# Attention scores of two heads at once: the queries' lo part as two 64-row tiles of PE

## The chip, the cores and the metric

The kernel runs on one core of a Trainium2 chip. Its time is the device time of one execution in microseconds; lower is better. A profile is one more execution, recorded by the hardware profiler. Engines are named as in the profile: PE is TensorE's matmul, PEld its weight load, DVE VectorE, ACT ScalarE, POOL GpSimd, SP the queue that issues most DMAs.

## The reference

Four batches, eight heads, 576 positions, head dimension 64. Attention has a bias that a small network makes from positions; after it come a dense layer pair and a layer of eight experts. Only the first function meets the change:

```python
def _attn_ref(q, k, v, w1, b1, w2):
    B, H, S, D = q.shape
    scores = np.matmul(q, k.transpose(0, 1, 3, 2)) / np.sqrt(D)
    ...                                   # bias from positions, [H, S, S]
    scores = scores + bias.transpose(2, 0, 1)[None, :, :, :]
    scores = scores - np.max(scores, axis=-1, keepdims=True)
    attn = np.exp(scores)
    attn = attn / (np.sum(attn, axis=-1, keepdims=True) + 1e-09)
    return np.matmul(attn, v).astype(np.float32)

def reference(**kwargs):
    ...
    x = attn_out.transpose(0, 2, 1, 3).reshape(B * S, H * D)
    x = _moe_ref(x=x, **moe_kwargs)       # x @ w_in, leaky relu, @ w_out
    return _moe2_ref(x=x, **moe2_kwargs)  # argmax over 8 experts, relu(x @ w1) @ w2
```

## The kernel before

**Precision.** An operand that must be exact to f32 is split into a hi part (rounded to f32r) and a lo part, the rest. A product then takes hi x hi, hi x lo and lo x hi. For scores, the two heads of a pair lie in one tile `kt` of 128 rows: head 0 has hi keys in rows 0 to 63 and lo keys in rows 64 to 127, head 1 the other way round. The queries stand twice, in rows 0 to 63 and again in rows 64 to 127, as `qhi` and `qlo`. One matmul over 128 rows with `qhi` therefore gives hi x hi and hi x lo at once; one with `qlo` gives lo x hi, and lo x lo besides.

**Steps.** Work is cut into 32 groups (batch, half of the queries, pair of heads) and these into 80 steps of 128 queries; the last step of every second group holds 64 queries of both heads (`ib == 4`, tile `qtail`). The other 64 are ordinary steps. A step's stages are spread over the loop of `phase1` (L638 to L682): while step n has its probabilities transposed (`transposes`, L450: tile `pst`; `transpose_tail`, L466: `psx`), the scores of step n + 2 are made. After a group's last step `values` (L485, tile `psv`) multiplies by the values, in column tiles of 64 (`tile_position=(0, 64 * h)`).

**Scores.** `scores(st, h)` (L392) makes one head: two column halves of 288 keys, each qhi then qlo, in a buffer `pss` of two PSUM banks. There are two such buffers (pool `psS`). One DVE instruction (L412) scales, adds the bias that already lies in `prob`, writes `prob` back and keeps the row's extreme in `stat`; `exps` (L417) is ACT's exponential, `normalise` (L425) the division, on POOL, DVE or ACT by a table.

**Fillers.** Between the stages stand units of other work, handed out by `Filler.run` against a quota of time: in the first eight steps the bias network (`bias_units`, L237, tile `psb`, column tiles of 32: four matmuls beside each other), then the up projection of the dense layers (`up_units`, L507, tile `psh`, twelve full matmuls a unit). `side` starts loads and conversions of later groups and of the dense layers' weights (`w_raw`, `wo_raw`, whose three bit operations run on DVE, L97 to L103).

**Order.** The program's text gives the order only roughly: the framework's scheduler sets each engine's list of instructions by priorities and readiness, so a change of a few lines moves many others. From the first matmul of the down projection (`psx` of L762) on, the lists of both kernels agree on PE.

What stands between two heads' scores in the loop is this:

```python
        if nx:
            at.scores(nx, 0)
        ...                              # normalise, side, half of the filler
        if st[3] != 4:
            at.transposes(st, 1)
        if nx and nx[3] != 4:
            at.scores(nx, 1)
```

Of the kernel before, what the change touches and what calls it, by code (L numbers as in the profile page):

```python
# [7 lines left out]
F32 = mybir.dt.float32  # L8
# [6 lines left out]
ALU = mybir.AluOpType  # L15
# [25 lines left out]
HALVES = ((0, 256, (0, 1)), (256, 320, (2, 3, 4)))  # L41
# [72 lines left out]
def new_w_in(p):  # L114
    return [p.tile([128, KD, FF // 2], F32R, name=f"wi{k}") for k in range(2)]
# [166 lines left out]
class Attention:  # L282
# [105 lines left out]
        self.prob[st] = (bt, e.small.tile([128, 2, 2], F32, tag="stat", name="stat"))  # L388

    def scores(self, st, h):  # L392
        nc, e = self.nc, self.e
        b, hf, p, ib = st
        kt = self.kv[b, p]
        hi, lo = self.qs[b, hf, p]
        tail = self.qtail[0]
        pr, stat = self.prob[st]
        ps = e.psS.tile([128, 2, 512], F32, tag="s", name="pss")
        o = 128 * (ib - HALVES[hf][2][0])  # L400
        if ib == 4:
            ops = [(tail[:, 256 * hh + 128 * k:][:, :128], 640 * hh) for hh in range(2) for k in range(2)]
        else:
            ops = [(t[:, h, o:o + 128], 576 * h) for t in (hi, lo)]
        for jh in range(2):
            for k, (lhsT, c0) in enumerate(ops):
                nc.tensor.matmul(  # L407
                    ps[:, jh, :288], lhsT=lhsT, rhs=kt[:, c0 + 288 * jh:][:, :288],
                    start=(k == 0), stop=(k == len(ops) - 1),
                )  # L410
        prv = pr[:, h].rearrange("p (a j) -> p a j", a=2)
        nc.vector.tensor_tensor_reduce(  # L412
            out=prv, in0=ps[:, :, :288], in1=prv,
            scale=-0.125, scalar=3.0e38, op0=ALU.add, op1=ALU.min, accum_out=stat[:, 0, h:h + 1],
        )

    def exps(self, st, h):  # L417
        nc = self.nc
# [134 lines left out]
def phase1(ctx, tc, e):  # L553

    nc = tc.nc
    early = tc.tile_pool(name="early", bufs=1, side="left")
    e.bout = early.__enter__()
    e.late = None
    at = Attention(nc, e)
    fl = Filler()  # L560
    groups = [(b, hf, p) for b in range(B) for hf in range(2) for p in range(NP)]
    steps = [g + (ib,) for g in groups for ib in HALVES[g[1]][2]]
    ns = len(steps)
    start = {}
    for n, st in enumerate(steps):
        start.setdefault(st[:3], n)


    todo = {}

    def put(n, pos, f, *args):
        todo.setdefault((max(n, 0), pos), []).append((f, args))

    def side(n, pos):
        for f, args in todo.pop((n, pos), ()):
            f(*args)

    for k, g in enumerate(groups):
        b, hf, p = g
        n0 = start[g]  # L580
        if k >= 2:
            put(n0 - 5, 1, at.q_load, g)
            put(n0 - 4, 1, at.q_hi, g)
            put(n0 - 3, 0, at.q_lo, g)
        if hf == 1:
            put(n0 - 3, 1, at.q_split_tail, g)
        if hf == 0 and k >= 2:
            m = n0 - 4 if b == 0 else start[b - 1, 1, p] + 3
            put(m, 0, at.kv_load, b, p)
            put(m, 1, at.kv_hi, b, p)  # L590
            put(m + 1, 0, at.k_lo, b, p)
            put(m + 3, 1, at.v_load, b, p)

    for k in range(2 * KF):
        put(3 + k // 2 if k < KF else 12 + (k - KF) // 2, k % 2, w_in_split, nc, e, k // 2, k % 2)
    for k in range(2 * KF):
        put(20 + k, k % 2, w_out_narrow, nc, e, k // 2, k % 2)

    bias_setup(nc, e)
    bu = bias_units(nc, e, WIDE)  # L600
    for k in range(32):
        if k == 20:
            for g in groups[:2]:
                at.q_load(g)
                at.q_hi(g)
                at.q_lo(g)
            for p in range(2):
                at.kv_load(0, p)
                at.kv_hi(0, p)
                at.k_lo(0, p)  # L610
                at.v_load(0, p)
        next(bu)
    fl.add(bu)
    for n in range(4):
        at.load_bias(steps[n])
    loaded = 4
    for n in range(2):
        for h in range(2):
            at.scores(steps[n], h)
            at.exps(steps[n], h)  # L620
    at.normalise(steps[0])

    xs = prev = None

    def values_out():
        nonlocal prev, xs
        if prev is None:
            return
        pb, ph, pp = prev
        if pp == 0:  # L630
            pool = e.xp if ph == 0 else e.late
            xs = [pool.tile([128, KD, HALVES[ph][1]], F32R, tag=f"x{i}{ph}", name=f"x{i}", bufs=1) for i in range(2)]
        at.x_split(prev, *xs)
        if pp == NP - 1:
            fl.add(up_units(nc, e, pb, ph, *xs))
        prev = None

    for n, st in enumerate(steps):  # L638
        g = st[:3]
        b, hf, p = g  # L640
        first = start[g] == n
        last = st[3] == HALVES[hf][2][-1]

        quota = 40 * 800.0 / 6.5 if n < 8 else KF * 1600.0 / 8 if hf == 0 else (13 if b == 0 else 17) * 1280.0 / 12
        nx = steps[n + 2] if n + 2 < ns else None
        while loaded < ns and at.free:
            at.load_bias(steps[loaded])
            loaded += 1
        if first:
            at.new_group()  # L650
        at.transposes(st, 0)
        values_out()
        at.transpose_tail(st)
        if nx:
            at.scores(nx, 0)
        if n + 1 < ns:
            at.normalise(steps[n + 1])
        side(n, 0)
        fl.run(quota / 2)
        if nx:  # L660
            at.exps(nx, 0)
        if st[3] != 4:
            at.transposes(st, 1)
        if nx and nx[3] != 4:
            at.scores(nx, 1)
        side(n, 1)
        at.done(st)
        if n == 7:
            fl.drain()
        else:  # L670
            fl.run(quota / 2)
        if nx and nx[3] != 4:
            at.exps(nx, 1)
        if last:
            at.pop_group(g)
            if n == 7:
                early.__exit__(None, None, None)
                e.late = ctx.enter_context(tc.tile_pool(name="late", bufs=1, side="left"))
                e.wi.append(new_w_in(e.late))
                at.free.append(PROBS)  # L680
            at.values(g)
            prev = g  # L682
    at.x_split(prev, *xs)
    fl.add(up_units(nc, e, prev[0], prev[1], *xs))
    return fl
# [661 lines left out]
def program(tc, e):  # L1347
# [4 lines left out]
    with ExitStack() as top:  # L1352
# [16 lines left out]
        for n, b in (("const", 1), ("big", 1), ("small", 4), ("raw", 1), ("kvp", 1), ("ptp", 1)):  # L1369
            setattr(e, n, pool(wide, n, b, side="right"))  # L1370
        e.psS, e.psT = (pool(wide, n, 2, space=PSUM) for n in ("psS", "psT"))
        tail = phase1(up, tc, e)
        wide.close()

# [60 lines left out]
```

## Time and profile before

| | |
|---|---|
| time, median of 3 | 1046.42 us (1045.34 to 1050.05) |
| profiled execution | 1049.75 us |
| its span, first to last instruction | 1047.9 us |
| granted clock of TensorE, mean | 0.988 of 2.4 GHz |
| PE, PEld busy | 997.3 us (95%), 815.7 us (78%) |
| DVE, ACT, POOL busy | 720.7 us (69%), 469.5 us (45%), 162.8 us (16%) |
| score matmuls qhi, qlo (L407) | 256 each, 81.0 us and 72.5 us busy |
| DVE on scores (L412) | 144, 107.9 us busy |

The page of a profile gives the busy time of each engine, the costliest groups of instructions and the chain of work that ended last. Busy time of PE counts overlapping matmuls once, and a matmul's duration includes its way through the array; what a matmul costs in a row of others is the distance from its start to the next start. Idle time of an engine costs only where that engine is the one waited for. Therefore the rows below are mostly of stretches and of single places, not of the whole span.

### The profile page before, as it was taken

The page shows a single profiled execution, that of the slowest core. Times are in us where ns is not written, and L with a number is a line of the kernel's source. Part 1 is how long each engine was busy: PE and PEld are TensorE (multiplying, and loading weights), DVE is VectorE, ACT ScalarE, POOL GpSimd, SP SyncE. Part 2 cuts the span into 40 slices and gives each one's busy share as a digit, 9 for nine tenths or more (in the row PEclk, how much of TensorE's full clock was granted, in tenths as well). Part 3 has the DMA queues.
Part 4 walks back from the last instruction along what each step waited for, and adds up shares of the span by engine and source line. Part 5 has one row for each costly group of instructions (what it writes and reads, how often), then busy time and mean ns, then how long its engine had stood idle before and what let it go on. Part 6 is the DMA issues. An engine that isn't in the chain of part 4 may idle for free.

```text
span 1047.9 us, 19304 instructions
## 1 busy us (share of the span) xinstructions
PE 997.3 (95%) x6330; PEld 815.7 (78%) x6330; DVE 720.7 (69%) x1842; ACT 469.5 (45%) x953; POOL 162.8 (16%) x204
## 2 busy tenths in 40 slices
PE   5999988999989999999999999999999999999995
PEld 2455777898878887998888888887777888888884
DVE  8878899888988899667745776588875156313312
ACT  6778665443433333333344333344452356424422
POOL 3232455000111112101000000000002111111210
PEclk9999999999999999999999999999999999999998
DMA  7877788887788466545267433437305148313410
GB/s 226 243 223 213 237 265 273 262 244 205 216 250 273 142 198 218 154 138 158 92 238 230 152 117 102 121 110 255 108 21 193 59 174 289 125 42 96 154 41 22
DMA packets 142466, 180.16 MB, mean 172 GB/s; under 512 B 20610, under 2 KB 94722, under 8 KB 142227
## 3 DMA queue, kind: packets, MB, share of 16 engines
q1 hardware_dynamic: 120418, 149.31, 46.6%
q10 hardware_dynamic: 18576, 19.03, 5.2%
q0 software_dynamic: 3360, 10.49, 2.9%
q8 instruction: 52, 0.85, 0.3%
q14 instruction: 60, 0.48, 0.1%
HBM read 196.18 MB, written 43.94 MB: 229 GB/s over the span
## 4 chain that ended last, share of the span: by engine, by line
PE 66%; DVE 14%; DMA 13%; issue 4%; ACT 1%; POOL 1%; SPq 0%; ACTq 0%; DVEq 0%; POOLq 0%
PE psx L762 12%; PE psh L519 11%; PE pu L1250 10%; PE pd L1281 10%; PE pss L407 5%; PE psv L494 5%; PE pst L458 4%; DMA g<-h 4%; PE psb L264 4%; DMA w_raw<-in_w_in_dram 2%; DMA prob<-bias 2%; DMA wo_raw<-in_w_out_dram 2%; PE pt L1261 1%; DMA qraw<-in_q_dram 1%; DVE prob L412 1%
## 5 line engine op out<-in xcount | busy, mean ns | idle before, releaser
L519 PE MATMUL psh<-x,wi 128*128 128x256 f32 (+1 forms) x1536 | 231.1, 300 | 3.9 <-ACT hst L68 1.3
L519 PEld LDWEIGHTS psh<-x,wi 128*128 128x128 f32 x1536 | 214.4, 192 | 6.6 <-ACT hst L68 2.2
L420 ACT ACTIVATE prob<-prob,stat 128x576 f32<-128x576 f32 x144 | 111.5, 775 | 187.2 <-DVE stat L412 168.3
L762 PE MATMUL psx<-woh,gh 128*128 128x512 f32 x288 | 114.0, 396 | 0.0
L762 PE MATMUL psx<-wol,gh 128*128 128x512 f32 x288 | 113.4, 394 | 0.0
L762 PE MATMUL psx<-woh,gl 128*128 128x512 f32 x288 | 113.0, 392 | 0.0
L412 DVE CUSTOM_DVE_ANT_0 prob<-pss,prob 128x576 f32<-128x576 f32 x144 | 107.9, 750 | 6.0 <-PE pss L407 3.6
L458 PE MATMUL pst<-ident,prob 128*128 128x128 f32 x576 | 91.3, 281 | 9.3 <-DVE pth L76 4.1
L68 ACT ACTIVATE gh<-g 128x512 fp32r<-128x512 f32 x72 | 45.4, 631 | 121.9 <-PE psx L762 110.6
L458 PEld LDWEIGHTS pst<-ident,prob 128*128 128x128 f32 x576 | 66.6, 141 | 30.1 <-issue 13.5
L76 DVE COPY pth<-pst 128x512 f32<-128x512 f32 (+1 forms) x120 | 74.7, 633 | 14.5 <-PE pst L458 13.7
L407 PE MATMUL pss<-kt,qhi 128*128 128x288 f32 x256 | 81.0, 332 | 1.3 <-DVE stat L412 1.3
L264 PE MATMUL psb<-mk,cf 128*32 128x79 f32 (+47 forms) x640 | 60.4, 408 | 14.2 <-POOL cf L248 6.8
L68 ACT ACTIVATE hst<-psh 128x256 f32<-128x256 f32 (+1 forms) x128 | 51.2, 400 | 49.2 <-PE psh L519 43.3
L494 PE MATMUL psv<-pth,vs 128*64 128x256 f32 (+1 forms) x512 | 72.8, 413 | 0.4 <-DVE pth L76 0.4
L407 PE MATMUL pss<-kt,qlo 128*128 128x288 f32 x256 | 72.5, 298 | 0.0
L745 DVE SCALAR_TENSOR_TENSOR g<-g 128x512 f32<-128x512 f32 x72 | 49.3, 689 | 33.5 <-DMA g<-h 33.2
L1281 PE MATMUL pd<-w2h,hth 128*128 128x512 f32 x160 | 67.8, 424 | 4.4 <-ACTq L1206 4.4
L80 DVE TENSOR_TENSOR htl<-pt,hth 128x512 fp32r<-128x512 f32 x40 | 27.1, 690 | 57.8 <-ACT hth L68 57.8
L1250 PE MATMUL pu<-w1h,xh 128*128 128x512 f32 x160 | 65.1, 407 | 0.3 <-ACT xh L68 0.3
L80 DVE TENSOR_TENSOR gl<-g,gh 128x512 fp32r<-128x512 f32 x72 | 49.5, 688 | 22.3 <-ACT gh L68 20.1
L1281 PE MATMUL pd<-w2h,htl 128*128 128x512 f32 x160 | 64.7, 404 | 0.0
(227 smaller groups left out, 1880.3 us busy)
## 6 DMA issues: line engine op xcount, KB each, us to landing
ws<-in_mw_dram SPq DMA_DIRECT2D x164, 512.0 KB
prob<-bias SPq DMA_DIRECT2D x64, 288.0 KB
g<-h SPq DMA_DIRECT2D x72, 256.0 KB
prob<-bias SPq DMA_DIRECT2D x64, 256.0 KB
bias<-bt SPq DMA_DIRECT2D x36, 295.5 KB
h<-hst ACTq DMA_DIRECT2D x64, 160.0 KB
w_raw<-in_w_in_dram SPq DMA_DIRECT2D x32, 256.0 KB
h<-hst ACTq DMA_DIRECT2D x64, 128.0 KB
```

The source lines that it names most:

```text
L68: nc.scalar.activation(out=out, in_=in_, func=AF.Copy)
L80: nc.vector.tensor_tensor(out=out, in0=x, in1=hi.bitcast(F32), op=ALU.subtract)
L264: nc.tensor.matmul(ps[32 * q:32 * q + 32, :b - a], lhsT=cf[:, 4 * (m % COEF_M) + q], rhs=x, start=True, stop=True, tile_position=(0, 32 * q),)
L407: nc.tensor.matmul(ps[:, jh, :288], lhsT=lhsT, rhs=kt[:, c0 + 288 * jh:][:, :288], start=(k == 0), stop=(k == len(ops) - 1),)
L412: nc.vector.tensor_tensor_reduce(out=prv, in0=ps[:, :, :288], in1=prv, scale=-0.125, scalar=3.0e38, op0=ALU.add, op1=ALU.min, accum_out=st ...
L420: nc.scalar.activation(out=pr[:, h], in_=pr[:, h], func=AF.Exp, bias=stat[:, 0, h:h + 1], scale=-1.0, accum_out=stat[:, 1, h:h + 1],)
L458: nc.tensor.transpose(ps[:, 128 * c:128 * c + 128], pr[:, h, 64 * h + 128 * c:][:, :128], e.ident)
L494: nc.tensor.matmul(ps[64 * h:64 * h + 64, :n], lhsT=vs[:, c, h], rhs=ph[:, h, c, :n] if c < 4 else pt[:, :n], start=(c == 0), stop=(c == 4 ...
L519: nc.tensor.matmul(ps[:, :n], lhsT=w[:, kc], rhs=x[:, kc, :n], start=(k == 0), stop=(k == 3 * KD - 1),)
L762: nc.tensor.matmul(ps, lhsT=a[:, c % 4], rhs=w[:, c], start=(k == 0), stop=(k == 3 * KF - 1))
L1250: nc.tensor.matmul(ps, lhsT=a[:, k], rhs=w[:, k, c], start=(i == 0), stop=(i == 3 * KD - 1))
L1281: nc.tensor.matmul(ps, lhsT=a[:, k], rhs=w[:, k], start=(k == 0 and j == 0), stop=(k == 7 and j == 2))
```

## The change

`scores(st)` now makes both heads of a step. It takes both `pss` buffers at once and issues four full matmuls with `qhi` (head 0, then head 1, two halves each). Then it issues the four products with `qlo`, each over 64 rows only: those rows that hold the head's hi keys, 0 to 63 for head 0 and 64 to 127 for head 1, given as `tile_position=(64 * h, 0)`. The heads alternate, so two neighbours use different rows of PE and different PSUM banks. The product lo x lo is no longer computed. Number of matmuls and number of columns are as before. In the loop the second head's scores move up, ahead of the first half of the filler and of `transposes(st, 1)`.

```diff
-    def scores(self, st, h):
+    def scores(self, st):
...
-        ps = e.psS.tile([128, 2, 512], F32, tag="s", name="pss")
-        o = 128 * (ib - HALVES[hf][2][0])
+        nh = 1 if ib == 4 else 2
+        pss = [e.psS.tile([128, 2, 512], F32, tag="s", name="pss") for _ in range(nh)]
...
-            ops = [(t[:, h, o:o + 128], 576 * h) for t in (hi, lo)]
-        for jh in range(2):
-            for k, (lhsT, c0) in enumerate(ops):
-                nc.tensor.matmul(
-                    ps[:, jh, :288], lhsT=lhsT, rhs=kt[:, c0 + 288 * jh:][:, :288],
-                    start=(k == 0), stop=(k == len(ops) - 1),
-                )
...
+            o = 128 * (ib - HALVES[hf][2][0])
+            for h in range(2):
+                for jh in range(2):
+                    nc.tensor.matmul(
+                        pss[h][:, jh, :288], lhsT=hi[:, h, o:o + 128], rhs=kt[:, 576 * h + 288 * jh:][:, :288],
+                        start=True, stop=False,
+                    )
+            for jh in range(2):
+                for h in range(2):
+                    r = slice(64 * h, 64 * h + 64)
+                    nc.tensor.matmul(
+                        pss[h][:, jh, :288], lhsT=lo[r, h, o:o + 128], rhs=kt[r, 576 * h + 288 * jh:][:, :288],
+                        start=False, stop=True, tile_position=(64 * h, 0),
+                    )
+        for h in range(nh):
+            prv = pr[:, h].rearrange("p (a j) -> p a j", a=2)
+            nc.vector.tensor_tensor_reduce(
+                out=prv, in0=pss[h][:, :, :288], in1=prv,
+                scale=-0.125, scalar=3.0e38, op0=ALU.add, op1=ALU.min, accum_out=stat[:, 0, h:h + 1],
+            )
...
         if nx:
-            at.scores(nx, 0)
+            at.scores(nx)
...
-        if nx and nx[3] != 4:
-            at.scores(nx, 1)
```

The order on PE after a group's values, in the later part of attention. `psv` are values, `pst` and `psx` transposes, `pss` scores, `psh` the up projection; the numbers are a matmul's output. Before:

```order
L494 MATMUL psv<-ptt,vs 64x256 x2
L458 MATMUL pst<-ident,prob 128x128 x4
L480 MATMUL psx<-ident,prob 128x128
L407 MATMUL pss<-kt,qhi 128x288
L407 MATMUL pss<-kt,qlo 128x288
L407 MATMUL pss<-kt,qhi 128x288
L407 MATMUL pss<-kt,qlo 128x288
L519 MATMUL psh<-x_3427,wi_77 128x320
```

and now:

```order
L509 MATMUL psv<-ptt,vs 64x256 x2
L473 MATMUL pst<-ident,prob 128x128 x4
L495 MATMUL psx<-ident,prob 128x128
L414 MATMUL pss<-kt,qhi 128x288 x4
L421 MATMUL pss<-kt,qlo 128x288 x4
L534 MATMUL psh<-x_3427,wi_1527 128x320
```

Where one head's four matmuls alternated, both heads' eight now stand together, hi first; the other head's scores are gone from behind the next transposes. In the first eight steps, between the bias tiles, the order before (buffer numbers kept; `pss_573` is head 0 of a step):

```order
L407 MATMUL pss_573<-kt_387,qhi_375 128x288
L407 MATMUL pss_573<-kt_387,qlo_377 128x288
L407 MATMUL pss_573<-kt_387,qhi_375 128x288
L407 MATMUL pss_573<-kt_387,qlo_377 128x288
L264 MATMUL psb_617<-mk_534,cf_614 32x272
```

and now, `pss_574` being head 1 of the same step:

```order
L264 MATMUL psb_655<-mk_631,cf_620 32x303
L414 MATMUL pss_574<-kt_387,qhi_375 128x288 x2
L421 MATMUL pss_574<-kt_387,qlo_377 128x288 x2
L264 MATMUL psb_655<-mk_639,cf_620 32x303
L264 MATMUL psb_655<-mk_641,cf_620 32x303
```

Here the scheduler has kept the heads apart: both lo matmuls of head 1 follow each other in the same rows of PE, with bias tiles on both sides.

## Rows read from the trace of the kernel before

**Rows 1.** The page: span, and busy time of each engine.
```profile
span 1047.9 us, 19304 instructions
PE 997.3 (95%) x6330; PEld 815.7 (78%) x6330; DVE 720.7 (69%) x1842; ACT 469.5 (45%) x953; POOL 162.8 (16%) x204
```

**Rows 2.** Stretches: length, busy PE, PEld, DVE, ACT, POOL; clock, DMA, GB/s.
```profile
30.00:110.00 80.00, 79.24 (x677) 40.09 (x678) 66.44 (x182) 62.44 (x144) 25.42 (x33) 1.00 0.77 223
110.00:330.00 220.00, 203.58 (x1509) 178.42 (x1509) 197.02 (x544) 104.69 (x250) 55.15 (x80) 0.98 0.81 248
330.00:535.00 205.00, 203.69 (x1573) 181.66 (x1570) 161.05 (x441) 74.47 (x184) 24.09 (x29) 1.00 0.54 160
```

**Rows 3.** Chain of waits by line: 110 to 330 us, then 330 to 535.
```profile
by line: PE psh L519 14.1%; DMA w_raw<-in_w_in_dram 8.5%; DMA wo_raw<-in_w_out_dram 7.2%; issue 7.1%; DMA qraw<-in_q_dram 5.8%; PE pst L458 5.3%; DVE prob L412 5.1%; PE pss L407 5.0%; DMA prob<-bias 4.2%; DMA kraw<-in_k_dram 4.1%; PE psv L4
...
by line: PE psh L519 39.8%; PE psv L494 15.9%; PE pss L407 14.5%; PE pst L458 13.3%; DMA h<-hst 3.2%; DVE prob L436 1.8%; issue 1.8%; DVE pth L76 1.7%; DVE prob L412 1.7%; DMA prob<-bias 1.5%; DVE kt L80 1.5%; PE psx L480 1.3%; DVE kt L76 0
```

**Rows 4.** Tile pss, 110 to 330 us: count, duration ns min/median/max, first and last start.
```profile
L407 PE MATMUL pss<-kt,qhi x112: 288/296/399, 116.0 to 326.1; 128*128 128x288 f32 x112
...
L407 PE MATMUL pss<-kt,qtail x63: 288/295/378, 110.3 to 282.7; 128*128 128x288 f32 x63
```

**Rows 5.** The same, 330 to 535 us.
```profile
L407 PE MATMUL pss<-kt,qhi x104: 292/296/381, 332.1 to 514.9; 128*128 128x288 f32 x104
```

**Rows 6.** Timeline of PE, 106.0 to 107.5 us: start, length of the merged row, instruction.
```profile
106.04 0.65 PE L494 MATMUL psv<-pth,vs 128*64 128x256 f32 x2
106.62 0.40 PE L407 MATMUL pss<-kt,qhi 128*128 128x288 f32 x1
106.86 0.29 PE L407 MATMUL pss<-kt,qlo 128*128 128x288 f32 x1
106.99 0.29 PE L407 MATMUL pss<-kt,qhi 128*128 128x288 f32 x1
107.12 0.29 PE L407 MATMUL pss<-kt,qlo 128*128 128x288 f32 x1
107.25 0.29 PE L407 MATMUL pss<-kt,qtail 128*128 128x288 f32 x1
107.48 0.44 PE L494 MATMUL psv<-pth,vs 128*64 128x256 f32 x2
```

**Rows 7.** Timeline of PE, 455.8 to 461.6 us.
```profile
456.05 0.60 PE L458 MATMUL pst<-ident,prob 128*128 128x128 f32 x4
...
458.88 1.95 PE L494 MATMUL psv<-pth,vs 128*64 128x256 f32 x16
460.65 0.60 PE L494 MATMUL psv<-ptt,vs 128*64 128x256 f32 x4
461.19 0.66 PE L458 MATMUL pst<-ident,prob 128*128 128x128 f32 x4
```

**Rows 8.** Timeline of PEld, 106.6 to 107.2 us.
```profile
106.62 0.19 PEld L407 LDWEIGHTS pss<-kt,qhi 128*128 128x128 f32 x1 [0.39 <-issue]
106.73 0.19 PEld L407 LDWEIGHTS pss<-kt,qlo 128*128 128x128 f32 x1
```

**Rows 9.** Waits of DVE, 110 to 330 us: total us, times, longest.
```profile
DVE prob L412 <- PE pss L407: 2.1, 4, 0.8
```

**Rows 10.** Waits of PE, 110 to 330 us.
```profile
PE pss L407 <- DVE stat L412: 1.1, 1, 1.1
```

**Rows 11.** Timeline of PE, 481.6 to 482.5 us.
```profile
481.80 0.60 PE L458 MATMUL pst<-ident,prob 128*128 128x128 f32 x4
482.23 0.28 PE L476 MATMUL psx<-ident,prob 128*64 128x128 f32 x1
482.27 0.38 PE L407 MATMUL pss<-kt,qhi 128*128 128x288 f32 x1
482.48 0.29 PE L407 MATMUL pss<-kt,qlo 128*128 128x288 f32 x1
```

**Rows 12.** Timeline of PEld, 458.6 to 459.2 us.
```profile
458.87 0.41 PEld L494 LDWEIGHTS psv<-pth,vs 128*64 128x64 f32 x6 [0.19 <-issue]
```

More of the change, by code (lines that the diff above doesn't have):

```diff
@@ L398, in scores @@
         pr, stat = self.prob[st]
-        ps = e.psS.tile([128, 2, 512], F32, tag="s", name="pss")
-        o = 128 * (ib - HALVES[hf][2][0])
+        nh = 1 if ib == 4 else 2
+        pss = [e.psS.tile([128, 2, 512], F32, tag="s", name="pss") for _ in range(nh)]
         if ib == 4:
             ops = [(tail[:, 256 * hh + 128 * k:][:, :128], 640 * hh) for hh in range(2) for k in range(2)]
-        else:
-            ops = [(t[:, h, o:o + 128], 576 * h) for t in (hi, lo)]
-        for jh in range(2):
-            for k, (lhsT, c0) in enumerate(ops):
-                nc.tensor.matmul(
-                    ps[:, jh, :288], lhsT=lhsT, rhs=kt[:, c0 + 288 * jh:][:, :288],
-                    start=(k == 0), stop=(k == len(ops) - 1),
-                )
[L411 to L415, printed above, removed]
+            for jh in range(2):
+                for k, (lhsT, c0) in enumerate(ops):
+                    nc.tensor.matmul(
+                        pss[0][:, jh, :288], lhsT=lhsT, rhs=kt[:, c0 + 288 * jh:][:, :288],
+                        start=(k == 0), stop=(k == len(ops) - 1),
+                    )
+        else:
+            o = 128 * (ib - HALVES[hf][2][0])
[5 more added lines that the diff above has]
+                    )
+            for jh in range(2):
+                for h in range(2):
+                    r = slice(64 * h, 64 * h + 64)
+                    nc.tensor.matmul(
+                        pss[h][:, jh, :288], lhsT=lo[r, h, o:o + 128], rhs=kt[r, 576 * h + 288 * jh:][:, :288],
[6 more added lines that the diff above has]
+                scale=-0.125, scalar=3.0e38, op0=ALU.add, op1=ALU.min, accum_out=stat[:, 0, h:h + 1],
+            )
     def exps(self, st, h):
@@ L617, in phase1 @@
     for n in range(2):
+        at.scores(steps[n])
         for h in range(2):
-            at.scores(steps[n], h)
             at.exps(steps[n], h)
```

## The prediction

> **What bounds the kernel now.** I read the totals first. PE is busy 95% of a span of 1047.9 us, DVE 69% [rows 1]. A mean over phases with different limits does not say what a score matmul is worth, so I next took the engines' busy time in the three stretches in which scores are computed. From 30 to 110 us PE is busy 79.2 of 80 us. From 110 to 330 it is busy 203.6 of 220 while DVE is busy 197.0: two engines near full, and 16.4 us in which PE stands still. From 330 to 535 PE is busy 203.7 of 205 [rows 2]. After that no instruction of the change remains. The chain of waits agrees: between 110 and 330 us the score matmuls are 5.0% of it (11.0 us), behind DMA loads of 5.8 to 8.5% each, and between 330 and 535 us they are 14.5% [rows 3].
>
> How many steps lie where: an ordinary step has four matmuls of the queries' hi part, so 112 of them are 28 steps in the middle stretch and 104 are 26 steps in the late one [rows 4, 5]. The remaining 10 of 64 are early. The 16 steps of 64 rows (qtail) do not change.
>
> The time of one score matmul is its distance to the next start, not its duration, since matmuls overlap. Between 106.86 and 107.25 four of them start 0.13 us apart [rows 6]. An ordinary step now costs 8 x 0.13 = 1.04 us of PE.
>
> **What the change removes.** Four full matmuls of lo become two pairs of 64-row tiles. If the two of a pair run beside each other, a pair costs one slot, and a step saves 2 x 0.13 = 0.26 us. No row shows a row tile here, but column tiles stand close by: 16 matmuls of 128x64 over 256 f32 columns begin within 1.77 us, 0.11 each [rows 7]. A transpose of 128 f32 columns takes 0.60 us for four with their tail, and 0.11 from start to start, so 256 columns alone would want 0.22: the column tiles do run two at a time. I take the same for row tiles.
>
> **What it adds: changes of tile shape.** The same rows show that PE does not pass from full tiles to column tiles for free. I priced four pieces.
> - Entering: the last score matmul starts at 107.25, the first value matmul at 107.48, 0.23 instead of 0.13 [rows 6]. That is +0.10.
> - Loading afterwards: the score matmul that follows the value matmuls starts at 106.62, the next one at 106.86, 0.24 instead of 0.13 [rows 6]: its weights were not loaded beneath other work. In PE's load row the first two loads stand 0.11 apart with nothing between them [rows 8], which is the load itself. +0.10 for an f32r tile.
> - Leaving: the last two pairs of value matmuls start at 460.65 and the next transpose at 461.19, 0.54 us for two pairs at 0.22, so +0.10 [rows 7].
> - Loading after leaving: four transposes take 0.66 instead of 0.60 [rows 7], +0.06; for f32r it is the 0.10 above.
>
> A round trip to lo tiles and back thus costs 0.40 us where f32r matmuls follow, 0.36 where transposes follow. The saving of a step is 0.26. This is why I expect a loss.
>
> The Trainium skill, page "TensorEngine Tiling (Array Packing)", section "Key Properties", says that a change of tiling mode, as against a change of tile within a mode, drains the engine. The trace agrees for column tiles with the 0.10 us above; by the packing alone the sum would end at a gain, and with the drain at a loss. No run here shows the drain for row tiles.
>
> **The sum on PE.** From the order of the changed kernel I counted changes of shape (bias 32 columns, values 64 columns, lo 64 rows, everything else full).
> - Middle and late stretch, 54 steps: 61 entries to lo and 61 exits, since some steps are split by a transpose. Entries 61 x 0.20 = 12.2. Exits: 51 to f32r x 0.20, 10 to others x 0.16, 11.8. Together 24.0 us. Saved: 47 steps have both pairs intact, one has them apart but whole, six lose one pair to a transpose standing between; 102 pairs x 0.13 = 13.3. Net +10.7 us of PE, 0.20 a step: 5.5 in the middle, 5.2 late.
> - Early, 10 steps: scores already stand between bias tiles of 32 columns, so both orders switch often, 93 times before and 102 after: 9 x about 0.19 = 1.7. In six of the ten steps the scheduler puts both lo matmuls of one head together, so none runs beside a partner; only 5 pairs are left, 0.65. Net +1.0.
>
> What of it reaches the end? Early and late nothing else gives way, so I take 1.0 and 5.2 in full. In the middle scores on the chain (11.0 us) are 29% of what the 112 + 112 + 63 = 287 score matmuls cost there [rows 4] (287 x 0.13 = 37.3), so 0.29 x 5.5 = 1.6; its bounds are 0 (all in PE's 16.4 us of gaps) and 5.5. Sum +7.8 us.
>
> **Edits at nothing.** Head 1's scores move ahead of one filler unit. DVE's first eviction can then start about 0.6 us later, after seven matmuls and the switch instead of four matmuls. On DVE the normalising, the copies of transposes and the next eviction queue behind it, and ACT's exponentials after that; but DVE waited only 2.1 us for scores in the whole middle stretch, in 4 waits [rows 9], so the work in front of the eviction covers it. If that cover is gone, 28 x 0.6 = 17 us of DVE at the very most. Both score buffers are claimed at once, so a step's first matmul needs both evictions of the step before; before the change such a wait came to 1.1 us, once [rows 10], and the evictions now come back to back and earlier for head 1. The lo x lo product goes without cost or gain, since a 64-row matmul streams the same 288 columns. Loads on SP's queue, and POOL's normalising, swap by one or two places: I take 0, bounds 2 us either way.
>
> The profiled execution took 1049.75 us, 1.85 more than its span and 3.3 more than the median of 1046.42. The same +7.8 makes 1057.6 from the one and 1054.2 from the other. I forecast against the median: 1054.
>
> **Rivals.**
> 1. *Row tiles need no drain (faster).* For it: a transpose with only 64 active columns starts at 482.23, 0.43 us after the first of four full ones, so at their own 0.11, and the second score matmul behind it at 482.48, 0.25 later, which is 0.11 + 0.13 and nothing more [rows 11]. A smaller tile alone costs nothing; possibly only column tiles rearrange PE. Against: that tile stands at the usual place, while lo of head 1 begins at row 64. Then 13.3 is saved: 0.29 x 6.9 in the middle, 6.4 late, 0.65 early, 9.1 in all: 1037. It decides once a round trip costs under 0.26. The Trainium skill, page "TensorE: Matmul & The Clock Gate", "Part 3: Packing small matmuls", prices a pack at one matmul plus about 4 ns for each further tile and names no cost for entering it; taken alone that rule is this rival.
> 2. *Cheaper switching (no change).* PE drains both ways, but the loads of a row tile or of the tile after it slip under running work. Then a round trip is 0.20, 61 x 0.20 = 12.2 against 13.3, and the time stays at 1045 to 1049. For it: the transposes lose only 0.06 after a switch [rows 7]; against it, the 0.24 of an f32r tile [rows 6].
> 3. *The tiles do not run beside each other (the change does not do what it says).* Serial matmuls, or serial weight loads at 0.11 each [rows 8], give no saving: 24.0 on PE, 12.4 x 0.29 + 11.6 + 1.7 early = 16.9, so 1063, and 1072 if the middle passes it all on. For it: a row tile fills all 128 columns, so the two loads of a pair go to the same columns, which those of column tiles don't. Against it: six loads of column tiles take 0.41 us together, where one after another at 0.11 they would take 0.66 [rows 12], so loads of different tiles can overlap.
>
> **Chances and range.** Half a per cent, 5.2 us, is about what a measurement of this kernel can tell from no change. Forecast 50%, with its own bounds 1050 to 1059, so that 8 of the 50 fall within half a per cent; rival 2, 20%; rivals 1 and 3, 15% each. Faster 0.15, same 0.28, slower 0.57. The range 1040 to 1063 leaves out the better half of rival 1 and the worse half of rival 3, each under 10%.
>
> **What would show it.** Starts in a score block of the changed profile: four hi at 0.13, then about 0.23 to the first lo; its partner under 0.02 later; about 0.24 to the second pair; about 0.23 to the next full tile, whose successor is 0.10 late. A partner 0.13 later is rival 3, 0.13 everywhere rival 1. PE's busy time should stay at 203 to 205 of 205 where it is full, with the attention ending near 543 us where it now ends near 535. I am wrong if attention ends at the same time or sooner, or if the difference sits in DVE's waits for scores or after the attention, where no instruction moved.

## The result, and the profile after

The changed kernel takes 1054.76 us (median of 11 runs, 1051.38 to 1059.52) against 1046.42 us (median of 11, 1039.98 to 1053.85) on the same chip: a ratio of 1.0079, 95% interval 1.0056 to 1.0102. Run again beside the experiments it stood at 1.0108 (1.0075 to 1.0141). Weighted by these intervals the two give 1.0089, plus or minus 0.0019: 9.3 us slower. The forecast was 1054.0.

The page of its profiled execution (1052.74 us), the rows that answer to [rows 1]:

```profile
span 1050.9 us, 19302 instructions
PE 1006.1 (96%) x6330; PEld 805.4 (77%) x6330; DVE 719.2 (68%) x1842; ACT 467.1 (44%) x953; POOL 162.5 (15%) x204
```

PE issues as many instructions as before and is busy 8.8 us longer. The stretches of [rows 2], with the same columns:

```profile
30.00:110.00 80.00, 79.58 (x674) 39.06 (x674) 65.71 (x181) 62.62 (x144) 24.50 (x31) 1.00 0.76 219
110.00:330.00 220.00, 208.71 (x1521) 174.01 (x1520) 196.31 (x547) 104.84 (x252) 57.28 (x83) 0.98 0.81 248
330.00:535.00 205.00, 203.55 (x1544) 173.03 (x1541) 160.08 (x436) 69.42 (x177) 23.28 (x29) 1.00 0.52 158
```

The gaps of PE in the middle stretch have shrunk from 16.4 to 11.3 us. DVE and the clock are as before.

One step in the late part on PE's timeline (columns as in [rows 6]):

```profile
454.68 0.60 PE L473 MATMUL pst<-ident,prob 128*128 128x128 f32 x4
455.11 0.27 PE L495 MATMUL psx<-ident,prob 128*128 128x128 f32 x1
455.14 0.78 PE L414 MATMUL pss<-kt,qhi 128*128 128x288 f32 x4
455.85 0.54 PE L421 MATMUL pss<-kt,qlo 64*128 64x288 f32 x4
456.32 2.02 PE L534 MATMUL psh<-x,wi 128*128 128x320 f32 x12
458.17 0.60 PE L473 MATMUL pst<-ident,prob 128*128 128x128 f32 x4
```

A row's start minus the start of the row before is what the earlier group cost. Four hi matmuls cost 0.71 us, four lo tiles 0.47, twelve matmuls of the filler 1.85. PE's load row of the same step shows that the tiles of a pair load beside each other, four loads in 0.30 us where four full ones take 0.56, and that PE's loads stand still (the bracket: idle before) on the way into the tiles and out of them:

```profile
455.12 0.56 PEld L414 LDWEIGHTS pss<-kt,qhi 128*128 128x128 f32 x4
455.85 0.30 PEld L421 LDWEIGHTS pss<-kt,qlo 64*128 64x128 f32 x4 [0.17 <-issue]
456.31 1.76 PEld L534 LDWEIGHTS psh<-x,wi 128*128 128x128 f32 x12 [0.17 <-issue]
```

Waits of PE and DVE in the middle stretch, answering to [rows 9, 10]. DVE's waits for scores:

```profile
DVE prob L427 <- PE pss L421: 1.9, 2, 1.1
```

PE's waits for the evictions:

```profile
PE pss L414 <- DVE stat L427: 2.3, 3, 1.2
```

Neither is large enough to carry the loss.

### The profile page after: what moved, and what is told of

It is laid out like the page before. It is cut to its first block, busy times and chain, and to the rows that moved or that the text cites. A ratio compares the mean times of both kernels' runs of the same rounds, so it can differ in the third digit from the quotient of the medians.

```text
span 1050.9 us, 19302 instructions
## 1 busy us (share of the span) xinstructions
PE 1006.1 (96%) x6330; PEld 805.4 (77%) x6330; DVE 719.2 (68%) x1842; ACT 467.1 (44%) x953; POOL 162.5 (15%) x204
## 4 chain that ended last, share of the span: by engine, by line
PE 68%; DVE 14%; DMA 11%; issue 4%; ACT 1%; POOL 1%; SPq 0%; ACTq 0%; DVEq 0%; POOLq 0%
PE psh L534 13%; PE psx L775 13%; PE pu L1263 10%; PE pd L1294 10%; PE psv L509 5%; PE pst L473 4%; DMA g<-h 4%; PE psb L264 4%; PE pss L421 2%; PE pss L414 2%; PE pt L1274 2%; DVE prob L427 1%; DMA wo_raw<-in_w_out_dram 1%; DMA h<-hst 1%; DMA prob<-bias 1%
## 5 line engine op out<-in xcount | busy, mean ns | idle before, releaser
L534 PE MATMUL psh<-x,wi 128*128 128x256 f32 (+1 forms) x1536 | 236.2, 304 | 4.2 <-ACT hst L68 1.9
L534 PEld LDWEIGHTS psh<-x,wi 128*128 128x128 f32 x1536 | 211.2, 191 | 15.0 <-issue 8.4
L427 DVE CUSTOM_DVE_ANT_0 prob<-pss,prob 128x576 f32<-128x576 f32 x144 | 104.9, 753 | 10.4 <-PE pss L421 8.7
L473 PE MATMUL pst<-ident,prob 128*128 128x128 f32 x576 | 88.7, 279 | 5.1 <-DVE pth L76 1.9
L80 DVE TENSOR_TENSOR xl<-pt,xh 128x512 fp32r<-128x512 f32 x21 | 14.4, 690 | 73.2 <-ACT xh L68 73.2
L1294 PE MATMUL pd<-w2l,hth 128*128 128x512 f32 x160 | 63.8, 399 | 0.0
```

Of the source, the lines that this page charges most:

```text
L80: nc.vector.tensor_tensor(out=out, in0=x, in1=hi.bitcast(F32), op=ALU.subtract)
L427: nc.vector.tensor_tensor_reduce(out=prv, in0=pss[h][:, :, :288], in1=prv, scale=-0.125, scalar=3.0e38, op0=ALU.add, op1=ALU.min, accum_ou ...
L473: nc.tensor.transpose(ps[:, 128 * c:128 * c + 128], pr[:, h, 64 * h + 128 * c:][:, :128], e.ident)
L534: nc.tensor.matmul(ps[:, :n], lhsT=w[:, kc], rhs=x[:, kc, :n], start=(k == 0), stop=(k == 3 * KD - 1),)
L1294: nc.tensor.matmul(ps, lhsT=a[:, k], rhs=w[:, k], start=(k == 0 and j == 0), stop=(k == 7 and j == 2))
```

## The experiments

The changed kernel differs from the one before in two ways that have to be told apart: the shape of four matmuls in each step, and the order of everything else, which the framework's scheduler makes anew whenever the text changes. Theory A says the loss is the changes of shape, about 0.40 us for each round trip against 0.26 saved. Theory B says it is the order.

**Full lo in the new order.** The lo matmuls over 128 rows again; the instruction lists of the two kernels agree on all five engines, but for that shape.

```diff
-                        pss[h][:, jh, :288], lhsT=lo[r, h, o:o + 128], rhs=kt[r, 576 * h + 288 * jh:][:, :288],
-                        start=False, stop=True, tile_position=(64 * h, 0),
+                        pss[h][:, jh, :288], lhsT=lo[:, h, o:o + 128], rhs=kt[:, 576 * h + 288 * jh:][:, :288],
+                        start=False, stop=True,
```

> The changed kernel with one thing undone: the lo part is again a full matmul over 128 rows (lo x lo included), both heads still together and every engine's instructions in the very order of the changed kernel. Theory A (what the 64-row tiles cost is the changes of tile shape, 0.40 us a round trip against 0.26 us saved): PE is relieved by 10.7 us in the middle and late stretch, about 8 us reach the end, 1047 us (1043 to 1050), level with the kernel before. Theory B (the new order, both heads' scores at once and their evictions back to back, costs the time; the tiles are about even): it stays at 1055 us (1052 to 1058). In the trace A wants all eight starts of a step 0.13 us apart and the last values of attention near 527 us.

Measured 1.0041 (1.0015 to 1.0067) times the kernel before: between the two theories. The order costs about 4 us, the tiles the rest. The same step on its timeline:

```profile
456.41 0.60 PE L472 MATMUL pst<-ident,prob 128*128 128x128 f32 x4
456.84 0.27 PE L494 MATMUL psx<-ident,prob 128*128 128x128 f32 x1
456.87 0.78 PE L414 MATMUL pss<-kt,qhi 128*128 128x288 f32 x4
457.49 0.70 PE L420 MATMUL pss<-kt,qlo 128*128 128x288 f32 x4
458.03 1.93 PE L533 MATMUL psh<-x,wi 128*128 128x320 f32 x12
459.79 0.60 PE L472 MATMUL pst<-ident,prob 128*128 128x128 f32 x4
```

From start to start: hi 0.62, lo 0.54, filler 1.76. With tiles it was 0.71, 0.47, 1.85. The tiles save 0.07 us in their own place, and the groups on either side lose 0.09 each: a step costs 0.11 us more.

**Two round trips per step.** The tiles of the second half of the keys stand apart from those of the first, with two hi matmuls between; the lists of DVE, ACT, POOL and SP are those of the changed kernel.

```diff
-            for h in range(2):
-                for jh in range(2):
+            for jh in range(2):
+                for h in range(2):
                     ...                     # hi, full
-            for jh in range(2):
                 for h in range(2):
                     r = slice(64 * h, 64 * h + 64)
```

> The suspected cost doubled: each column half of the scores gets its own hi matmuls and then its own lo pair, so a step goes to 64-row tiles and back twice instead of once; same matmuls, same pairs, 413 changes of tile shape instead of 281. Theory A: 66 more round trips of 0.40 us, 26 us of PE; 26 of them late at full price (10.4 us), 28 in the middle at 0.29 to 1 of it (3 to 11 us), the rest early: 14 to 22 us over the changed kernel, 1069 to 1077 us. Theory B (order): no more than 3 us over the changed kernel, 1052 to 1058. A rival within A, that entering is hidden when the entries follow each other closely, would give 1060 to 1065.

Measured 1.0299 (1.0252 to 1.0347), 22.0 us (plus or minus 5.4) above the changed kernel (1.0299 - 1.0089, of 1047): the upper end of what Theory A called, and far from Theory B's 3 us. The list of instructions has 132 more changes of shape, 66 round trips: 0.33 us each (0.25 to 0.42) at the end of the program. On PE:

```profile
456.23 0.51 PE L414 MATMUL pss<-kt,qhi 128*128 128x288 f32 x2
456.68 0.40 PE L420 MATMUL pss<-kt,qlo 64*128 64x288 f32 x2
457.00 0.54 PE L414 MATMUL pss<-kt,qhi 128*128 128x288 f32 x2
457.47 0.40 PE L420 MATMUL pss<-kt,qlo 64*128 64x288 f32 x2
457.80 2.03 PE L533 MATMUL psh<-x,wi 128*128 128x320 f32 x12
```

From the first hi to the filler 1.57 us pass where the changed kernel takes 1.18 (456.32 - 455.14): a round trip is 0.39 us of PE. Of that 0.33, or 85% (64 to 106%), arrives. This is the cost of a round trip, doubled and read off the total.

**Lo tiles of one head behind each other.** The order of the four tiles is 0, 0, 1, 1 instead of 0, 1, 0, 1.

```diff
-            for jh in range(2):
-                for h in range(2):
+            for h in range(2):
+                for jh in range(2):
                     r = slice(64 * h, 64 * h + 64)
```

> The pairs broken, the changes of shape kept: the two lo matmuls of head 0 come first, then those of head 1, so that at most the middle two of four lie beside each other; 281 changes of shape as in the changed kernel. Theory A: a step loses one to two slots of 0.13 us. If the middle two still overlap, one slot a step: 3.4 us late, 1 to 3.6 in the middle, 1058 to 1062 us; if none overlaps, twice that, 1062 to 1069. A theory that pairs bring nothing at the end, since something else takes the time: 1055 as the changed kernel.

Measured 1.0045 (1.0021 to 1.0069). The expectation fell: it is not slower than the changed kernel but, against all I had thought, faster.

**Scores straight from f32.** Each head's 64 x 64 products of unsplit queries and keys, four tiles beside each other, no hi and lo at all. It computes the scores from other operands, and other experts can then be chosen, so only its attention can be compared.

```diff
+                for c in ((h,) if ib == 4 else range(2)):
+                    q0 = o if ib == 4 else o + 64 * c
...
-                        pss[h][:, jh, :288], lhsT=lo[r, h, o:o + 128], rhs=kt[r, 576 * h + 288 * jh:][:, :288],
-                        start=False, stop=True, tile_position=(64 * h, 0),
+                        pss[h % nh][64 * c:64 * c + 64, jh, :288], lhsT=x[r, h, q0:q0 + 64],
+                        rhs=kt[r, 288 * jh:288 * jh + 288], start=True, stop=True, tile_position=(64 * h, 64 * c),
```

> Scores straight from f32: no hi and lo parts of queries and keys at all; each step is eight f32 matmuls over 64 rows into 64 columns of PE (head by rows, half of the 128 queries by columns), four beside each other, one round trip of shapes a step. Sum by Theory A: two groups of four at 0.24 us (f32 columns take twice an f32r column, as the value matmuls show) plus 0.40 for the round trip, 0.88 us a step against 1.04 before and 1.24 in the changed kernel; late 26 x -0.16 = -4 us against the kernel before. Besides, 50 us of splitting leave DVE (24 us kt lo, 10 kt copies, 11 qlo, 5 qtail), about half of it in the middle stretch where DVE stood at 197 of 220 us; there PE's 16 us of gaps can close. 1025 to 1042 us. If the four do not run beside each other (0.24 each, 2.3 us a step): slower than 1060. If f32 in these tiles takes four passes: 1.36 us a step, 1040 to 1055.

Measured 1087.83 us. Its last value matmuls start at 552.8 us, where the kernel before has them at 530.1, so the attention alone is 23 us slower. On PE:

```profile
457.47 0.27 PE L437 MATMUL psx<-ident,prob 128*128 128x128 f32 x1
457.67 1.20 PE L363 MATMUL pss<-kt,qraw 64*64 64x288 f32 x16
458.80 2.03 PE L476 MATMUL psh<-x,wi 128*128 128x320 f32 x12
```

From the last transpose to the filler 1.33 us pass, 0.20 of them before the first tile; the changed kernel takes 1.21 (456.32 - 455.11). The expectation of 1025 to 1042 us fell. The row holds 16 matmuls for the program's eight, so the trace has each f32 product twice: four groups of four (they start at 457.67, 457.96, 458.21 and 458.45, within 0.02 us inside a group) where I had reckoned with two. That is near the 1.36 us of the expectation's last case, although the time lies outside its 1040 to 1055. Dropping the lo parts gains nothing on PE. Not followed further.

**Only head 1's scores moved up.** The kernel before, all matmuls full, one buffer claimed at a time.

```diff
         if nx:
             at.scores(nx, 0)
+        if nx and nx[3] != 4:
+            at.scores(nx, 1)
...
-        if nx and nx[3] != 4:
-            at.scores(nx, 1)
```

> The kernel before, with one edit: head 1's scores are made right behind head 0's, ahead of the filler and of the transposes of head 1. All matmuls stay full, hi and lo alternate within a head, and a head claims its buffer only when its own turn comes. The run with full lo in the changed order stood about 4 us above the kernel before. If the move of head 1 is what costs (theory B1: the transposes of the step before come later and DVE gets two evictions back to back), this one stands about 4 us above too, 1050 to 1054. If the grouping costs (theory B2: all four hi matmuls of both heads first, so the first matmul needs both buffers and no eviction can begin before the sixth matmul), it stays within 1.5 us of the kernel before. If the order costs nothing and the earlier run was scatter (theory B0), this run and the repeated full-lo run both stay within 1.5 us of it.

Measured 0.9984 (0.9964 to 1.0003). The move, in the order that the scheduler made of it, costs nothing. That order is again one of its own, so a cost of the move and a gain of the order could still hide each other.

**The full-lo kernel and the changed kernel once more**, beside each other.

> The changed order with lo as full 128-row matmuls once more, now on the same chip as the changed kernel itself, to divide the loss between order and tiles. Theory B (order): 3 to 5 us above the kernel before. Theory A (changes of shape alone): within 1.5 us of it, and 6 to 10 us below the changed kernel. Second trace: attention should end 2 to 5 us later than in the kernel before if the order costs, with waits of PE for the evictions (stat) above the 1.1 us of before.

> The changed kernel, on the same chip as the full-lo version. If the tiles cost half of the loss, it stands 3 to 5 us above the full-lo version; if the shapes are the whole loss, 7 to 10; if the order is the whole loss, within 1.5. PE should be busy 6 to 8 us longer than in the full-lo version up to the end of attention.

Measured 1.0035 (1.0006 to 1.0063) and 1.0108 (1.0075 to 1.0141). The order costs again, the tiles again on top. Beside each other the tiles' price is 0.0073 (0.0044), 7.6 us, which is in the band that I had called for the shapes alone, and yet the full-lo kernel too stands above the one before. PE is busy 411.9 us against 403.3 from 110 us to the last values (8.6 more, called 6 to 8). With full lo the last values start at 532.8 us, 2.7 later than before, and PE waits 1.9 us for evictions, both as Theory B had it. With both runs of each: order 1.0038 (plus or minus 0.0019), tiles 1.0089 - 1.0038 = 0.0051 (0.0027), 5.3 us.

**Both heads' scores down.** The changed kernel with `scores(nx)` at head 1's old place, behind `transposes(st, 1)`, and head 0's exponentials behind it.

```diff
-        if nx:
-            at.scores(nx)
...
-        if nx:
-            at.exps(nx, 0)
         if st[3] != 4:
             at.transposes(st, 1)
+        if nx:
+            at.scores(nx)
+            at.exps(nx, 0)
```

> The changed kernel, but both heads' scores now stand at head 1's old place, behind the first half of the filler and the transposes of head 1, and head 0's exponentials behind them. The tiles and their changes of shape stay. If being early or late in the step is what the order costs (theory B1), this moves the time by 2 us or more against the changed kernel: down, because transposes are no longer held back, or up, because the exponentials then start later and DVE and ACT wait. If only the grouping and the shapes count, it stays within 2 us of the changed kernel, 1053 to 1057.

Measured 1.0171 (1.0136 to 1.0207); the medians stand 5.9 us above the changed kernel's run beside it (1066.0 and 1060.1). Waits of PE, 110 to 535 us:

```profile
PE pst L473 <- DVE pth L76: 8.6, 9, 2.5
PE pst L473 <- POOL prob L453: 5.4, 5, 2.4
PE psx L495 <- POOL prob L453: 2.2, 3, 1.7
```

The first two in the changed kernel:

```profile
PE pst L473 <- DVE pth L76: 1.9, 3, 0.8
PE pst L473 <- POOL prob L453: 0.3, 1, 0.3
```

The transposes now wait for probabilities (`prob`, normalised by POOL) that start later, 7.6 us instead of 0.3, and longer for DVE's copies of transposes (`pth`). So this place is no better, and nothing here speaks against scores early in the step. How much of the 5.9 us is the place is not shown, since this kernel's lists differ from the changed kernel's on all five engines.

**Lo first, with tiles and with full matmuls.** The step begins with the four lo products, then hi of head 0, then hi of head 1, so that head 0 is complete earlier.

```diff
+            for jh in range(2):
+                for h in range(2):
+                    ...                     # lo, start=True, stop=False
             for h in range(2):
                 for jh in range(2):
-                    ...                     # hi, start=True, stop=False
-            for jh in range(2):
-                for h in range(2):
-                    ...                     # lo, start=False, stop=True
+                    ...                     # hi, start=False, stop=True
```

> The changed kernel with lo and hi exchanged in a step: the two pairs of lo tiles first, then the two hi matmuls of head 0, then the two of head 1. Head 0 is complete after the fourth slot of PE instead of the sixth, head 1 after the last, so the two evictions can follow each other with PE still at work, and the changes of shape are as many as before. If the order costs because the evictions start late and the next scores wait for both buffers (theory B3), this recovers the greater part of the 4 us of order: 4 to 6 us above the kernel before, and waits of PE for the evictions fall from 2.3 us to about 1. If the order costs through something else (its transposes, its loads), it stays at 8 to 11 us above.

> The same order, lo first, with lo as full 128-row matmuls: eight slots of 0.13, head 0 complete after the sixth, head 1 after the eighth. Theory B3: within 2 us of the kernel before. Theory of order through something else: 3 to 5 us above, as the full-lo run with hi first. Against the run with lo tiles in the same order it should be 4 to 7 us faster by either theory, which is the price of the shapes alone.

Measured 1.0067 (1.0042 to 1.0092) with tiles, 0.9983 (0.9956 to 1.0009) with full matmuls. With full matmuls the cost of the order is gone: 5.8 us below the full-lo kernel with hi first (1.0038 - 0.9983 = 0.0055, plus or minus 0.0033). The tiles' price is 0.0084 (0.0037) here, 8.8 us, above the 4 to 7 called. Theory B3 had the time of the full version right, while the version with tiles, 7.0 us above the kernel before, lies between its two bands. But its mechanism does not show. PE's waits for the evictions, 110 to 535 us, should have fallen to about 1; with tiles, then with full matmuls:

```profile
PE pss L415 <- DVE stat L427: 2.6, 3, 1.3
PE pss L414 <- DVE stat L426: 5.8, 4, 2.2
```

Neither is below the changed kernel's 2.3, and the faster of the two kernels waits longer. A step with tiles, then one with full matmuls:

```profile
458.74 0.27 PE L495 MATMUL psx<-ident,prob 128*128 128x128 f32 x1
458.94 0.53 PE L415 MATMUL pss<-kt,qlo 64*128 64x288 f32 x4
459.40 0.80 PE L421 MATMUL pss<-kt,qhi 128*128 128x288 f32 x4
460.03 1.92 PE L534 MATMUL psh<-x,wi 128*128 128x320 f32 x12
```

```profile
458.60 0.27 PE L494 MATMUL psx<-ident,prob 128*128 128x128 f32 x1
458.62 0.78 PE L414 MATMUL pss<-kt,qlo 128*128 128x288 f32 x4
459.24 0.70 PE L420 MATMUL pss<-kt,qhi 128*128 128x288 f32 x4
459.78 1.91 PE L533 MATMUL psh<-x,wi 128*128 128x320 f32 x12
```

1.29 us against 1.18 from the last transpose to the filler: again 0.11 a step, although the tiles now stand at the other end of the block.

**Heads apart once more.**

> The changed kernel with the lo tiles of head 0 first and those of head 1 behind (0, 0, 1, 1) once more. Its block took PE as long as the changed kernel's (466 and 464 ns from the first lo to the next full tile), yet its first run stood only 4.7 us above the kernel before, the changed kernel's two runs 8 and 11. If an earlier eviction of head 0 is worth that (B3), it stands 4 to 6 us above again; if the first run was scatter, 8 to 11.

Measured 1.0047 (1.0020 to 1.0074), so the first run was no scatter: with both, 1.0046 (0.0018), 4.5 us below the changed kernel. But the reason is not the earlier eviction. Its step on PE:

```profile
458.16 0.27 PE L495 MATMUL psx<-ident,prob 128*128 128x128 f32 x1
458.19 0.78 PE L414 MATMUL pss<-kt,qhi 128*128 128x288 f32 x4
458.90 0.54 PE L421 MATMUL pss<-kt,qlo 64*128 64x288 f32 x4
459.37 2.02 PE L534 MATMUL psh<-x,wi 128*128 128x320 f32 x12
```

The four tiles cost the same 0.47 us, and in 47 of 48 recorded blocks both signals to DVE stand on the third and fourth tile to start, where the changed kernel has them: PE has paired the heads by itself, and head 0 is complete no earlier. It is not the scheduler's doing, as far as the trace shows: the fourth tile's signal is an addition (`+=`) in these 47 blocks, which fits a tile issued between the two signals, where in 45 of the changed kernel's 48 it is a step of one (`++`).

**Two orders, each with and without tiles.** The built instruction lists show which kernels belong together. On DVE, ACT, POOL and SP, and on PE when hi and lo are not told apart, the last three kernels (lo first with tiles, lo first full, heads apart) are identical among themselves. So are the changed kernel and its full-lo version, but the two lists differ. An example from SP's queue in the middle of attention, from the first list to the second:

```
 L339 DMA qraw<-in_q_dram 128x2x256
-L122 DMA w_raw<-in_w_in_dram 128x2x256
+L312 DMA vs<-in_v_dram 128x640
+L122 DMA w_raw<-in_w_in_dram 128x2x256 x2
 L383 DMA prob<-bias_60 128x576
-L122 DMA w_raw<-in_w_in_dram 128x2x256
 L385 DMA prob<-bias_60 128x512
 L386 DMA prob<-bias_60 128x64
-L312 DMA vs<-in_v_dram 128x640
```

| ratio to the kernel before | full lo | lo tiles |
|---|---|---|
| first order (the changed kernel's) | 1.0038 (0.0019) | 1.0089 (0.0019) |
| second order | 0.9983 (0.0027) | 1.0046 (0.0018) and 1.0067 (0.0025) |

Read across, tiles cost 5.3 (plus or minus 2.8), 6.6 (3.4) and 8.8 us (3.9). Read down, the first order costs 5.8 us (3.5) with full matmuls and 4.5 (2.7) or 2.3 (3.3) with tiles; the 2.3 is not clear of its noise.

The busy time of PE scatters less than the totals. From 110 us to the start of the last value matmuls (columns as in [rows 2]), the changed kernel, the same order with full lo, and lo first full:

```profile
110.00:533.00 423.00, 410.26 (x3048) 345.43 (x3048) 355.41 (x981) 174.26 (x429) 80.56 (x112) 0.99 0.67 205
```

```profile
110.00:533.90 423.90, 403.04 (x3041) 354.69 (x3039) 352.57 (x977) 173.42 (x429) 79.89 (x109) 0.99 0.67 204
```

```profile
110.00:527.60 417.60, 401.54 (x3034) 353.36 (x3034) 349.48 (x975) 173.08 (x427) 78.32 (x109) 0.99 0.68 207
```

Over the profiles of kernels with full lo and with one round trip a step, both heads' scores down left out (416.8), PE is busy 402.4, 401.6, 403.0, 403.3 and 401.5 us with full lo (before, head 1 moved up, full lo twice, lo first full) and 410.3, 411.9, 412.4, 413.1 and 412.8 with one round trip (changed kernel twice, heads apart twice, lo first): 9.7 us more in the mean, 7.9 in the first order and 11.2 in the second. Its idle time in the same stretch is 18.7 us in the mean of the first five and 14.9 in the second. So in the mean 3.8 of the 9.7 us fall into gaps, and 5.9 arrive at the end of attention. The 5.9 is known to plus or minus 3.9 only, since two profiles of one kernel differ by up to 8 us in this stretch.

## Why the prediction was right, point by point

**The pieces of a change of shape: right.** Starts in the changed trace: hi to hi 0.13 us, hi to the first lo 0.22, partner 0.003 to 0.004 later, pair to pair 0.235, lo to the next full tile 0.22, and that tile's successor late by 0.10. All were called. So was the argument from column tiles, that a pair costs one slot, if f32 is compared with f32. Two kinds of rows of the changed kernel, values in column tiles and the filler in full tiles, both over 256 columns:

```profile
474.32 1.95 PE L509 MATMUL psv<-pth,vs 128*64 128x256 f32 x16
476.09 0.60 PE L509 MATMUL psv<-ptt,vs 128*64 128x256 f32 x4
478.65 1.68 PE L534 MATMUL psh<-x,wi 128*128 128x256 f32 x12
```

Eight pairs take 1.77 us, 0.22 each, and partners start 7 ns apart (474.583 and 474.590). Of the full matmuls twelve take 1.68 with their tail, some 0.12 each. That does not make the pair two slots, for the kernel holds the filler's operands in f32r and those of the values in f32. The f32 transposes, 128 columns in 0.11, give 0.22 for 256 f32 columns, as the prediction had it. The measured round trip is 0.39 us (two round trips per step), called at 0.40; an intact step loses 0.11 of PE, called at 0.40 - 0.26 = 0.14. The Trainium skill's "TensorEngine Tiling (Array Packing)", "Key Properties", which has a change of tiling mode drain the engine, is borne out for row tiles: 0.22 from the last hi to the first lo against 0.13 between two hi matmuls. The Trainium skill's page "TensorE: Matmul & The Clock Gate", "Part 3: Packing small matmuls", agrees on the 3 to 4 ns between partners, and taken alone would have given the wrong sign.

**The rivals.** Rival 1 (no drain) and rival 2 (loads slip under running work) fall with the 0.22 and with the late successor; rival 3 (no overlap) with four loads in 0.30 us and two partners 4 ns apart.

**PE's sum: right in size.** Called +10.7 us for the middle and late part. The changed kernel's two profiles have PE busy 8.7 us longer than the kernel before up to the last values, 7.9 longer than full lo in the same order.

**What of it reaches the end: the late term was mis-sized, the rest is known roughly.** The late term was 5.2 us. I had spread the 10.7 evenly, 0.20 a step, while the steps that the scheduler splits lie earlier. From the end of the 19th group's values (344.0 us in the changed kernel) to the last values, 24 ordinary steps, it takes 189.0 and 189.4 us in its two profiles and 186.5 and 186.9 with full lo: 2.5 us, nearly the 24 times 0.11 of intact steps, so practically all of it is passed on. Early, the end of the fourth group's values comes 1.2 to 1.5 us later than with full lo (109.9 in both profiles against 108.4 and 108.7), called 1.0. What is left for the middle is 5.3 - 2.5 - 1.3 = 1.5 us in this order (1.6 called). But the 5.3 is uncertain by 2.8, and in the second order the tiles cost 6.6 and 8.8 in all, so this agreement shows little. The rule that I used there, the 29% that scores have on the chain, is not confirmed: of 66 further round trips 85% arrive. Nor is it refuted. With 0.39 us in full for the 38 early and late trips and 29% of it for the 28 in the middle the sum would be 18.0 us, inside 22.0 plus or minus 5.4. PE's idle time is down to 9.1 us with two trips a step, which suggests that the first microseconds find a gap and later ones less often.

**"Edits at nothing": wrong for the order.** I allowed 2 us either way for SP's loads and POOL. Moving head 1's scores shows no cost (-1.7 us, interval -3.8 to +0.3). Claiming both buffers at once need not cost either, since the second order does so and stands at 0.9983. But the order that the scheduler made costs 4.0 us (2.0 to 6.0) with all matmuls full. None of my rivals named it: it is the term that the sum put at nothing. So part of the total's fit may be luck: by the runs of this order the tiles cost 5.3 us where I had 7.8, and the order 4.0 where I had 0. The second is an error. The first need not be one, since 7.8 lies within 5.3 plus or minus 2.8.

**What would show it.** The end of attention was a poor witness. It came at 533.0 us in the first profile and at 540.9 in the second, against 530.1; called 8 us later. Single executions differ that much in the middle: from the fourth group's values to the 19th's the two profiles of the changed kernel take 234.1 and 241.6 us. Even behind attention, where no instruction moved, the profiles with hi and lo scores differ, 514 to 521 us. Only the timed runs could decide.

**What stays open.** That the order alone costs some 4 to 6 us is shown by two pairs of kernels with the same matmuls (in the pair with full matmuls hi and lo also change places within a step). Which of the moved instructions does it is not. It can be neither the late steps (186.6 us from the end of the 19th group's values with lo first full, 186.5 and 186.9 with full lo in the first order) nor head 0's earlier completion (heads apart, same signals). The fourth group's values end 0.6 to 0.9 us earlier in the second order (107.8). By elimination the rest lies in the middle stretch, where DVE is busy nearly 90% of the time (196.3 of 220 us); but there the profiles of one kernel differ by more than what is sought.

## What to carry to other kernels

Price a change of PE's tile shape by the whole round trip (in, load, out, load: 0.39 us here) and set it against the slots that the packing frees (0.13 each): two freed slots a trip lose, and by these prices more than three would be needed (not tried). Gather packed work until it outweighs the trip, or leave it full. And where a scheduler orders the program, a rewrite of a few lines carries an order of its own, worth some half a per cent here: compare the instruction lists, and build the same shape in a second order, before crediting the edit.

## What the runs showed of the hardware that I had not expected

Row tiles of PE need not be neighbours in the program to run beside each other. Issued 0, 0, 1, 1, the first two starts stand 7 ns apart, the second pair follows 0.234 us later and carries both heads' completion signals; the four cost 0.47 us in either order. Where two tiles of one head stand alone, as in early steps, they start 0.24 us apart.

And the first pair after a change of shape is the dear one. The tile rows of lo in the late stretch (columns as in [rows 4]):

```profile
L421 PE MATMUL pss<-kt,qlo x104: 287/393/401, 331.7 to 516.3; 64*128 64x288 f32 x104
```

The duration is near 0.40 us for a first pair and near 0.29 for a second. The first pair's load starts only with it (455.85 both, on PEld and PE), so the 0.11 is taken to be that load. One pair alone costs 0.32 to 0.33 us to the next full tile (457.00 - 456.68 and 457.80 - 457.47 with two round trips), two cost 0.47: the second adds 0.14 to 0.15, about one slot of 0.13. So row tiles do pair at one slot once PE is in their shape.
